# Weight loads of channels 64 apart, contiguous selection and a carry on either engine in a kernel of a long convolution and a routed two-token FFN

## The chip, the cores and the metric

The kernel runs on one core of one Trainium2 chip. The metric is the time of one execution on the device in microseconds (us), the median of several runs. A profile is one further execution, taken by the hardware profiler. Engines: PE multiplies matrices (PEld loads its weights, PEq is its sequencer), DVE and ACT do elementwise work, POOL and SP here mostly issue DMAs; SPq and ACTq are the queues on which SP and ACT issue theirs. L947 means line 947 of the kernel before.

## The reference

Cut to what matters; all arrays are bf16, x is 2048 tokens of 512 channels.

```python
g = sigmoid((x * gate_w).sum(-1, keepdims=True))
# A: a state-space layer, 512 channels of 128 states each
dt = exp(log_dt)[:, None]; A = A_re + 1j*A_im; B = B_re + 1j*B_im; C = C_re + 1j*C_im
l = arange(2048).astype(bf16)                       # lags are rounded to bf16
P = exp((dt * A)[:, :, None] * l[None, None, :])
K = einsum("dn,dnl,dn->dl", C, P, dt * B).real
a = causal_convolution(x, K) + x * Dskip            # over tokens, by channel
# B: the two tokens with the largest r go through a gated FFN
r = x @ w_r; idx = argsort(-r)[:, :2]; xs = x[idx]
b = x;  b[idx] += ((silu(xs @ w_gate) * (xs @ w_up)) @ w_down) * sigmoid(r[idx])
out = g * a + (1 - g) * b
```

## The kernel before, in words

The convolution runs in the frequency domain, over two blocks (b = 0, 1) of 1024 tokens and two halves (h = 0, 1) of HC = 256 channels. Its steps, with the lines of the profile:

- **Head.** The parameters are loaded; `scaled` (L598) multiplies them on PE by a diagonal of exp(log_dt). The results that it writes `wide` (AL and tb) have channels in natural order in PSUM: four matmuls, each writing every fourth column. DVE makes from them the phases (TMP1, TMP2, B16) and the products of B and C (CM1, CM2, WW). The first DVE operation that needs the last parameter, B_im, is CM1. `warm` (L640) is filler work on PE.
- **Tokens.** x is loaded (U), transposed (XT) and folded, and `forward` (L947) multiplies it by the tables F to get its spectrum X. The routing and the FFN (L813 to L912) lie between; a scatter by POOL (L916) adds its result to a copy of x in the output tensor, from which U is loaded again later.
- **Tables.** The exponential of A dt times a lag is a product of one of 32 factors (t1) and one of NJ = 21 factors (t2). `tab1` builds the first (TP, sines by ACT at L471 in eight passes per half; `quarter`, `first` and `step` on PE prepare their angles, and one `SCL`, L479, negates the sine of each of four angle groups); `tab2` the second (RW), on DVE.
- **Taps.** `kgen` (L966) multiplies, for four channels at a time, a weight load of 32 t1 x 4 channels with 21 t2 x 4 channels, 64 such groups per half. Of the 4 x 4 pairs of channels only the equal ones are wanted. Groups are gathered in PSUM and copied to KA (`EV`, L475) in pieces of 12, 12, 8, 12, 12 and 8 groups; KA has a group's 21 x 4 columns side by side.
- **Selection.** `sel` and `sel2` (L978 to L994) pick the equal channels: for each of the four channels of a group (c4) a matmul with columns of an identity reads every 84th element of KA (64 of them, or two sets of 64) and writes every fourth column of PSUM, on four 32-column tiles of PE side by side. L982 adds the rows of Dskip and of the FFN; L994 takes a few edge taps. The result, KC, is in natural channel order.
- **Spectra.** `kspec` (L1015) multiplies KC by tables KP, giving KK for tap block i = 0 (four matrices u) and i = 1 (one). Block 1 needs a carry: block 0's spectrum is added, or subtracted. For the first half PE adds it by matmuls behind the product (L1017, chosen by `CARRY = (0,)`); for the second, ACT writes it into PSUM ahead of the product (L1009).
- **Products and inverse.** DVE multiplies X by KK and combines (L460, `products`; for one part PE adds, L1053). `inverse` (L1100) turns the result back, into PSUM banks which ACT has filled with the skip term (L1078); L1110 and L1118 scale the result into U, which goes out by DMA.

What sets the order: no engine schedules itself. `ORDER` is one list of all operations, by three-digit numbers in base 36 in the order in which the program defines them; each engine runs its own in that order and waits by semaphores for what they depend on, DMA issues included. `SECOND` has a digit for each operation that can run on either of two engines (`EV`, `SCL` and others), `PLACES` the PSUM bank or buffer of each short-lived tile. The `cost=` figures have no effect on the running kernel.

## Time and profile before

| | us |
|---|---|
| median of 3 runs (151.97 to 153.57) | 152.06 |
| the profiled execution | 150.95 |
| its span, first to last instruction | 149.1 |
| busy in it: PE / PE weight loads | 140.9 / 104.1 |
| busy in it: DVE / ACT / POOL | 137.8 / 127.1 / 30.1 |

The span is shorter than the execution by what lies before the first and after the last instruction. A row of a timeline is start, duration, engine, line, operation, out<-in, count, and in brackets the idle time ahead of it with what ended it; neighbours on one engine overlap by some 0.1 us, since the pipeline takes the next before the last has drained. A row of a group is line, engine, operation, shapes, count, then busy us and mean ns of one, then idle time ahead and its causes. A row of the chain of waits is start, us, and what ran or was waited for. TensorE had its full clock (mean granted clock 0.996).

### The profile page before, as it was taken

To read this page: it belongs to the slowest core of one execution; us is meant where nothing else is said; L and a number is where in the kernel's file an instruction comes from. 1 tells how busy PE (TensorE), PEld (TensorE's weight loads), DVE (VectorE), ACT (ScalarE), POOL (GpSimd) and SP (SyncE) were. 2 spreads that over 40 slices of the span, in tenths; PEclk is the share of its full clock that TensorE was granted. 3 is DMA by queue.
4 is the path that set the end of the run, shared out by engine and by line. 5 is a ranking of instruction groups with operands and counts; after the bars stand their busy time and mean duration, and the time that the engine had idled before them with its cause. 6 is when DMAs were issued, how large, how long until landed. Compare 5 with 4: busy or idle time off the path is not lost.

```text
span 149.1 us, 3990 instructions
## 1 busy us (share of the span) xinstructions
PE 140.9 (94%) x1717; PEld 104.1 (70%) x1733; DVE 137.8 (92%) x192; ACT 127.1 (85%) x198; POOL 30.1 (20%) x11
## 2 busy tenths in 40 slices
PE   7889998999999999999989999999999999999990
PEld 2767755486664445968747879987886688888880
DVE  0699998999999999999999699999999999999982
ACT  3497989999999999999996986595999999999521
POOL 2000200000000999999930000000000000000000
PEclk9999999999999999999999999999999999999998
DMA  4899599919900004000491000558920011114314
GB/s 130 264 320 373 160 407 429 364 27 303 457 7 0 0 4 141 0 4 0 110 418 45 0 0 4 156 180 321 392 87 0 4 35 39 46 29 141 104 37 141
DMA packets 12499, 21.16 MB, mean 142 GB/s; under 512 B 1175, under 2 KB 8354, under 8 KB 12322
## 3 DMA queue, kind: packets, MB, share of 16 engines
q1 hardware_dynamic: 11474, 20.26, 38.7%
q10 hardware_dynamic: 976, 0.66, 1.4%
q8 instruction: 13, 0.21, 0.6%
q14 instruction: 4, 0.03, 0.1%
q0 software_dynamic: 32, 0.00, 0.0%
HBM read 18.81 MB, written 4.20 MB: 154 GB/s over the span
## 4 chain that ended last, share of the span: by engine, by line
PE 69%; ACT 13%; DVE 10%; DMA 4%; issue 1%; SPq 1%
PE ps L1100 18%; PE ps L947 14%; PE ps L966 8%; DVE AR L460 8%; PE ps L1015 7%; ACT AR L475 5%; ACT AR L471 5%; PE ps L699 3%; PE ps L978 3%; DMA AR<-in_A_B_im_dram 3%; PE ps L892 2%; DMA AR<-in_A_log_dt_dram 2%; DVE AR L475 2%; PE ps L704 2%; PE ps L994 1%; PE ps L1053 1%
## 5 line engine op out<-in xcount | busy, mean ns | idle before, releaser
L460 DVE TENSOR_TENSOR AR<-AR 128x1024 bf16<-128x1024 bf16 (+8 forms) x135 | 118.1, 932 | 5.3 <-ACT AR L471 3.6
L475 ACT ACTIVATE AR<-ps 128x1024 bf16<-128x1024 f32 (+9 forms) x60 | 51.7, 880 | 9.4 <-PE ps L966 3.1
L916 POOL DMA_INDIRECT out_dram<-AR x1 | 27.8, 27805 | 32.2 <-DVE AR L464 32.2
L947 PE MATMUL ps<-AR 128*128 128x512 bf16 x121 | 29.3, 379 | 0.5
L471 ACT ACTIVATE AR<-ps 128x1024 bf16<-128x1024 int16 (+2 forms) x34 | 28.2, 871 | 1.7 <-PE ps L598 1.6
L1100 PE MATMUL ps<-AR 128*128 128x256 bf16 x256 | 29.4, 273 | 0.0
L1100 PEld LDWEIGHTS ps<-AR 128*128 128x128 bf16 x256 | 24.8, 98 | 3.7 <-DVE AR L460 0.4
L947 PEld LDWEIGHTS ps<-AR 128*128 128x128 bf16 x128 | 11.9, 97 | 12.5
L966 PEld LDWEIGHTS ps<-AR 128*128 128x128 bf16 x512 | 18.6, 96 | 1.9
L1015 PE MATMUL ps<-AR 128*128 128x256 bf16 x160 | 19.0, 273 | 0.0
L966 PE MATMUL ps<-AR 128*128 128x84 bf16 (+1 forms) x512 | 18.9, 196 | 0.0
L471 ACT ACTIVATE ps<-AR 128x256 f32<-128x256 bf16 (+1 forms) x36 | 17.8, 554 | 0.1
L1015 PEld LDWEIGHTS ps<-AR 128*128 128x128 bf16 x160 | 15.5, 98 | 2.5 <-ACT ps L471 0.4
L479 ACT ACTIVATE AR<-AR 128x256 int32<-128x256 f32 (+2 forms) x22 | 13.1, 635 | 0.1
L471 ACT ACTIVATE AR<-AR 128x1024 bf16<-128x1024 int16 (+4 forms) x12 | 9.4, 782 | 1.3 <-DMA AR<-in_A_log_dt_dram 1.3
L1110 ACT ACTIVATE AR<-ps,AR 128x256 bf16<-128x256 f32 x24 | 9.9, 490 | 0.0
L640 PE MATMUL ps<-AR 128*128 128x464 bf16 x22 | 6.7, 444 | 0.9 <-DVE AR L643 0.9
L460 DVE TENSOR_TENSOR AR<-AR,ps 128x2048 bf16<-128x2048 bf16 (+1 forms) x6 | 7.2, 1257 | 0.3 <-PE ps L598 0.3
L699 PE MATMUL ps<-AR 128*128 128x512 f16 x24 | 6.2, 380 | 0.0
L1118 ACT ACTIVATE AR<-ps,AR 128x256 bf16<-128x256 f32 x3 | 1.4, 474 | 5.1 <-PE ps L1100 4.2
L978 PE MATMUL ps<-AR 128*32 128x128 bf16 x64 | 4.7, 420 | 0.2 <-ACT AR L475 0.2
L475 DVE COPY AR<-ps 128x1024 bf16<-128x1024 bf16 (+1 forms) x8 | 4.8, 679 | 0.0
(76 smaller groups left out, 98.7 us busy)
## 6 DMA issues: line engine op xcount, KB each, us to landing
AR<-c_ksp SPq DMA_DIRECT2D x5, 512.0 KB, 4.9
AR<-in_A_u_dram SPq DMA_DIRECT2D x8, 256.0 KB, 5.0
AR<-out_dram SPq DMA_DIRECT2D x4, 512.0 KB, 7.1
AR<-c_inv SPq DMA_DIRECT2D x1, 2048.0 KB, 8.8
AR<-in_B_w_up_dram SPq DMA_DIRECT2D x1, 1792.0 KB, 7.0
AR<-in_B_w_gate_dram SPq DMA_DIRECT2D x1, 1792.0 KB, 14.1
out_dram<-AR SPq DMA_DIRECT2D x14, 128.0 KB, 2.2
AR<-c_fwd SPq DMA_DIRECT2D x2, 512.0 KB, 6.7
```

Of the source, the lines that this page charges most:

```text
L460: return P.op(DVE, lambda h: h.tensor_tensor(out=o, in0=a, in1=b, op=op), rd, wr, cost=tt_cost(o, a, b), **k)
L471: return P.op(ACT, lambda h: h.activation(out=o, in_=a, func=func, scale=scale, bias=bias), rd, wr, cost=0.185 + nel(o) * 0.833e-3 + (0.09 ...
L475: return P.op((ACT, DVE), (lambda h: h.activation(out=o, in_=a, func=ACTF.Copy), lambda h: h.tensor_copy(o, a)), rd, wr, cost=(0.185 + n * ...
L479: return P.op((ACT, DVE), (lambda h: h.activation(out=o, in_=a, func=ACTF.Copy, scale=c), lambda h: h.tensor_scalar(out=o, in0=a, scalar1= ...
L699: r = hh.matmul(pb(0, 128, b * 512, (1, 512)), TI(4), PC(0, 128, k * D + h * HC, (0, 2), (1, HC)), start=False, stop=True, skip_group_chec ...
L916: P.op(POOL, lambda h: h.indirect_dma_start(dr(out, 0, (D, L), (1, D)), bass.IndirectOffsetOnAxis(ap=IDX(0, 2, 0, (1, 1)), axis=0), ZB(0, ...
L947: last = h.matmul(pb(0, 128, j * 512, (1, 512)), F[ft](0, 128, (kt * 2 + 1 - j) * 128, (1, 128)), pm[q](0, 128, kt * 512, (1, 512)), start ...
L966: last = hh.matmul(pb(0, 128, g // k * 512 + g % k * W4 + o, (1, n)), TP[h][1 - i // 2](0, 128, (b0 + g) * 128, (1, 128)), r[i](0, 128, (b ...
L978: last = hh.matmul(pb(32 * k, 32, c4, (256, 2), (4, 64)), CB(0, 128, c4, (4, 32)), ka(c4, GROUPS[2 * bk][k], (16, 2)), start=(c4 == 0), st ...
L1015: last = hh.matmul(pb(0, 128, n * 256, (1, 256)), KP[u](0, 128, tau * 128, (1, 128)), KC[h](0, 128, jg * 256, (1, 256)), start=(k == 0 and ...
L1100: r = hh.matmul(pb(0, 128, e * 256, (1, 256)), G(0, 128, ((par * 2 + part) * 4 + ft) * 512 + (2 * t2 + e) * 128, (1, 128)), X(0, 128, h * ...
L1110: return [hh.activation(out=U(0, 128, tb * D + h * HC, (1, HC)), in_=pb(0, 128, tb // 2 % 2 * 256, (1, HC)), func=ACTF.Copy, scale=SG(0, 1 ...
```

## The change

- `scaled`, where `wide`: a half's channels are laid out in PSUM so that the four of a group (a weight load) are 64 apart in the half, not neighbours. All tables follow; `WT` makes the products WW in two operations per part instead of one, reading in the new order.
- `kgen`: eight pieces of eight groups instead of six; the copy to KA writes with a step of four elements, so that the rows of four groups lie side by side.
- `sel`, `sel2`: read runs of four elements, and write 64 contiguous columns. The Dskip and FFN rows are one matmul of 256 columns instead of four of 64.
- `kspec`: the carry is an operation of its own ahead of the product, on ACT or on PE for each of the eight cases. By the new list PE does two of the first half's four and three of the second's.
- The two loads of F (512 KB each) become four (256 KB each).
- A new list of all operations, with other choices of engine and place. Decoded, among others: the log_dt load is SP's first; DVE has five of the eight transposes' copies instead of six; both quarter turns of the first half's second table run on ACT; one of the four block-0 spectra of the first half and three of that half's four block-1 products come behind the first part of the second half's `kgen`; the first half's inverse takes block 0 before block 1.

```diff
-CARRY = (0,)
...
-            DQ([(F[2 * j](0, 128, 0, (1, 2048)), f_c[:, j * 2048:(j + 1) * 2048])], [], [F[2 * j], F[2 * j + 1]], 524288)
+            for f in (2 * j, 2 * j + 1):
+                DQ([(F[f](0, 128, 0, (1, 1024)), f_c[:, f * 1024:(f + 1) * 1024])], [], [F[f]], 262144)
...
-                        o = out(k, (4, 128)) if wide else out(k * 128, (1, 128))
+                        o = out(4 * k, (HC, 2), (1, 4), (16, 16)) if wide else out(k * 128, (1, 128))
...
-        n4 = lambda b, c: b(0, 128, c, (1, 128), (128, 4))
-        w4 = lambda b, c: b(0, 128, c, (4, 128), (1, 4))
+        def WT(p, b0, b1, op):
+            def f(hh):
+                r = None
+                for h in range(2):
+                    n4 = lambda b, c: b(0, 128, c + 64 * h, (1, 16), (128, 4), (16, 4))
+                    r = hh.tensor_tensor(out=WW(0, 128, p * D + h * HC, (1, HC)), in0=n4(*b0), in1=n4(*b1), op=op)
+                return r
+            P.op(DVE, f, [CM1, CM2], [(WW, p)], cost=1.38)
...
-        TT(w4(WW, 0), n4(CM1, 0), n4(CM2, D), ALU.subtract, [CM1, CM2], [(WW, 0)])
-        TT(w4(WW, D), n4(CM1, D), n4(CM2, 0), ALU.add, [CM1, CM2], [(WW, 1)])
+        WT(0, (CM1, 0), (CM2, D), ALU.subtract)
+        WT(1, (CM1, D), (CM2, 0), ALU.add)
...
-            for b0, ng in ((0, 12), (12, 12), (24, 8), (32, 12), (44, 12), (56, 8)):
+            for b0, ng in [(8 * i, 8) for i in range(8)]:
...
-                EV(KA[h](0, 128, b0 * W4, (1, ng * W4)), pb(0, 128, 0, (512, 2), (1, k * W4)), [pb], [(KA[h], b0)])
-            ka = lambda c4, j, *d: KA[h](0, 128, c4 + 4 * j, *d, (4 * NJ, 64))
+                EV(KA[h](0, 128, b0 * W4, (4 * W4, ng // 4), (1, 4), (4, W4)), pb(0, 128, 0, (512, 2), (1, k * W4)), [pb], [(KA[h], b0)])
+            ka = lambda c4, j, *d: KA[h](0, 128, (c4 + 4 * j) * 4, *d, (4 * W4, 16), (1, 4))
...
-                            last = hh.matmul(pb(32 * k, 32, c4, (256, 2), (4, 64)), CB(0, 128, c4, (4, 32)), ka(c4, GROUPS[2 * bk][k], (16, 2)),
+                            last = hh.matmul(pb(32 * k, 32, 64 * c4, (256, 2), (1, 64)), CB(0, 128, c4, (4, 32)), ka(c4, GROUPS[2 * bk][k], (64, 2)),
                                              start=(c4 == 0), stop=(c4 == 3 and bk + k > 0), tile_position=(0, 32 * k))
                     if bk == 0:
-                        for c4 in range(4):
-                            last = hh.matmul(pb(0, 32, c4, (4, 64)), CB(0, 128, 64, (1, 32)), ZB(0, 128, h * HC + c4, (4, 64)), start=False, stop=(c4 == 3), tile_position=(0, 0))
+                        last = hh.matmul(pb(0, 32, 0, (1, HC)), CB(0, 128, 64, (1, 32)), ZB(0, 128, h * HC, (1, HC)), start=False, stop=True, tile_position=(0, 0))
...
-                        last = hh.matmul(pb(32 * k, 32, c4, (4, 64)), CB(0, 128, c4, (4, 32)), ka(c4, GROUPS[4][k]), start=(c4 == 0), stop=(c4 == 3), tile_position=(0, 32 * k))
+                        last = hh.matmul(pb(32 * k, 32, 64 * c4, (1, 64)), CB(0, 128, c4, (4, 32)), ka(c4, GROUPS[4][k]), start=(c4 == 0), stop=(c4 == 3), tile_position=(0, 32 * k))
...
-                        last = hh.matmul(pb(0, 128, 256 + c4, (4, 64)), CB(0, 128, EK0 + (c4 * 2 + k) * 32 - 32, (1, 128)), ka(c4, 1 - k), start=False, stop=True, skip_group_check=True)
+                        last = hh.matmul(pb(0, 128, 256 + 64 * c4, (1, 64)), CB(0, 128, EK0 + (c4 * 2 + k) * 32 - 32, (1, 128)), ka(c4, 1 - k), start=False, stop=True, skip_group_check=True)
...
-                        pe = h in CARRY
-                        pb = psum(2, full=True, seed=i == 1 and not pe)
+                        pb = psum(2, full=True, seed=i == 1)
...
-                        if i and not pe:
-                            AC(pb(0, 128, 0, (1, 1024)), KK[h](0, 128, (1 - part) * 2048 + qd * 1024, (1, 1024)), ACTF.Copy, [ck], [pb], scale=1.0 - 2.0 * part)
+                        if i:
+                            kc = lambda m, n, part=part, qd=qd: KK[h](0, 128, (1 - part) * 2048 + qd * 1024 + m * 512, (1, n))
+                            def carry(hh, pb=pb, part=part, kc=kc):
+                                return [hh.matmul(pb(0, 128, m * 512, (1, 512)), CB(0, 128, 128 * part, (1, 128)), kc(m, 512), start=True, stop=False, skip_group_check=True) for m in range(2)][-1]
+                            def seed(hh, pb=pb, part=part, kc=kc):
+                                return hh.activation(out=pb(0, 128, 0, (1, 1024)), in_=kc(0, 1024), func=ACTF.Copy, scale=1.0 - 2.0 * part)
+                            P.op((ACT, PE), (seed, carry), [ck, CBI], [pb], cost=(0.185 + 1024 * 0.833e-3, 0.4314))
...
-                            for m in range(2 * i * pe):
-                                last = hh.matmul(pb(0, 128, m * 512, (1, 512)), CB(0, 128, 128 * part, (1, 128)), KK[h](0, 128, (1 - part) * 2048 + qd * 1024 + m * 512, (1, 512)), start=False, stop=True, skip_group_check=True)
```

More of the change, by code (lines that the diff above doesn't have):

```diff
@@ L397 @@
 )
 PLACES = (
[L399 removed]
+    "21044600176014706064110140224111440010012400106222606064020266000140240220010664642246010100000001010260606201160066220615052430260022023470456"
 )
@@ L1014, in ks @@
                                     jg = KUSE[u][1]
-                                    last = hh.matmul(pb(0, 128, n * 256, (1, 256)), KP[u](0, 128, tau * 128, (1, 128)), KC[h](0, 128, jg * 256, (1, 256)), start=(k == 0 and n % 2 == 0 and (pe or i == 0)), stop=(k == len(uses) - 1 and n % 2 == 1 and not (i and pe)), skip_group_check=(i == 1))
-                            for m in range(2 * i * pe):
-                                last = hh.matmul(pb(0, 128, m * 512, (1, 512)), CB(0, 128, 128 * part, (1, 128)), KK[h](0, 128, (1 - part) * 2048 + qd * 1024 + m * 512, (1, 512)), start=False, stop=True, skip_group_check=True)
+                                    last = hh.matmul(pb(0, 128, n * 256, (1, 256)), KP[u](0, 128, tau * 128, (1, 128)), KC[h](0, 128, jg * 256, (1, 256)), start=(k == 0 and n % 2 == 0 and i == 0), stop=(k == len(uses) - 1 and n % 2 == 1), skip_group_check=(i == 1))
                             return last
-                        P.op(PE, ks, [KP[u] for u in uses] + [(KC[h], KUSE[u][1]) for u in uses] + ([CBI, ck] if i and pe else []), [pb.buf], cost=4 * len(uses) * 0.1095 + 2 * i * pe * 0.2157)
+                        P.op(PE, ks, [KP[u] for u in uses] + [(KC[h], KUSE[u][1]) for u in uses], [pb.buf], cost=4 * len(uses) * 0.1095)
                         o = KK[h](0, 128, i * 4096 + part * 2048 + qd * 1024, (512, 2), (1, 512))
```

41 lines of the change are left out of this document (20 added, 21 removed).

## The prediction

> **What bounds the kernel now.** I read the busy time by stage first (columns: start and end of the stage, its length, then busy us of PE, of its weight loads, of DVE, ACT and POOL, the granted clock, DMA share, GB/s).
>
> ```profile
> 20.00:59.00 39.00, 38.08 (x403) 22.19 (x407) 38.35 (x74) 38.77 (x59) 10.77 (x1) 1.00 0.51 191
> 59.00:75.40 16.40, 15.87 (x286) 11.96 (x288) 16.40 (x25) 16.05 (x19) 16.40 (x1) 1.00 0.15 46
> 75.40:85.43 10.03, 9.91 (x109) 7.27 (x111) 8.86 (x12) 8.50 (x14) 0.63 (x1) 1.00 0.34 139
> 85.43:143.29 57.86, 57.60 (x701) 48.93 (x703) 57.31 (x57) 48.76 (x87) 0.52 (x1) 1.00 0.30 102
> ```
>
> Up to 75.4 all three compute engines are full; from there ACT has room, PE and DVE have none, and DVE's last product ends at 143.29. So nothing is won by easing one engine alone. Up to 75 the question is ACT's queue; behind it, whichever of PE and DVE ends later. Next I read the timelines at the joints, ACT first, then DVE.
>
> ```profile
> 15.16 1.02 ACT L475 ACTIVATE AR<-ps 128x1024 bf16<-128x1024 bf16 x1 [1.04 <-PE ps L797]
> 19.76 0.20 ACT L475 ACTIVATE AR<-ps 128x32 bf16<-128x32 f32 x1 [0.68 <-PE ps L820]
> 82.24 1.02 ACT L475 ACTIVATE AR<-ps 128x1024 bf16<-128x1024 f32 x1 [1.42 <-PE ps L1015]
> 83.16 1.02 ACT L471 ACTIVATE AR<-ps 128x1024 bf16<-128x1024 int16 x1
> 84.06 0.39 ACT L475 ACTIVATE AR<-ps 128x256 bf16<-128x256 f32 x1
> 84.33 1.07 ACT L479 ACTIVATE AR<-AR 128x1024 bf16<-128x1024 bf16 x1
> ```
>
> ```profile
> 8.51 1.22 DVE L460 TENSOR_TENSOR AR<-AR,ps 128x1024 f32<-128x1024 bf16 x1 [0.33 <-PE ps L598]
> 85.43 10.57 DVE L460 TENSOR_TENSOR AR<-AR 128x2048 bf16<-128x2048 bf16 x7 [1.17 <-ACT AR L479]
> ```
>
> The four ACT rows from 82.24 are neighbours: an operation costs its duration less about 0.1 (82.24 to 83.16 is 0.92). DVE's one large idle, 1.17 before 85.43, waits for the negated sine of the second half's last angle group (84.33), and ACT is late there because the evacuation ahead of it stood 1.42 waiting for PE. I call 85.43 the joint.
>
> **The head.** The log_dt load goes from third to first on SP's queue.
>
> ```profile
> 0.73 0.36 SPq L482 DMA_DIRECT2D AR<-c_bf  x1
> ```
>
> ```profile
> 1.65 2.57 DMA AR<-in_A_log_dt_dram
> 4.24 3.79 DMA AR<-in_A_B_im_dram
> 8.07 0.41 PE ps L598 x4
> ```
>
> It is issued 1.65 - 0.73 = 0.92 earlier, and so are the exp that waits for it and the B_im load that ACT issues behind that exp: landing at 7.1. But the new order puts both B groups behind that landing, not one (another 0.41). CM1 starts at 8.51 - 0.92 + 0.41 = 8.0: head 0.5, of which I take 0.4. The two halved F loads add two issues of about 0.4 on SP, ahead of the constants it loads next; PE meets F3 only behind the logits, so I cost this at nothing, and 0.8 if that cover fails. The "wide" results go to PSUM 64 bytes apart instead of 16.
>
> ```profile
> L598 PE MATMUL ps<-AR x24: 219/314/314, 5.2 to 8.3; 128*128 128x128 bf16 x24
> ```
>
> Spaced writes already cost 314 against 219 for the contiguous eight of the 24. I take no change; the bounds are 16 times 0.095 = 1.5 either way.
>
> **The selection (L978 to L994).** PE's rows for the first half, with matmuls to compare:
>
> ```profile
> 75.46 1.15 PE L978 MATMUL ps<-AR 128*32 128x128 bf16 x16 [0.15 <-ACT AR L475]
> 76.66 1.15 PE L978 MATMUL ps<-AR 128*32 128x128 bf16 x13
> 78.71 0.68 PE L991 MATMUL ps<-AR 128*32 128x64 bf16 x16
> 79.32 1.13 PE L994 MATMUL ps<-AR 128*128 128x64 bf16 x8
> 17.04 1.75 PE L813 MATMUL ps<-AR 128*128 128x2 bf16 x64
> 93.62 5.66 PE L966 MATMUL ps<-AR 128*128 128x84 bf16 x160
> ```
>
> ```profile
> L978 PE MATMUL ps<-AR 128*32 128x128 bf16 x64 | 4.7, 420 | 0.2 <-ACT AR L475 0.2
> L966 PE MATMUL ps<-AR 128*128 128x84 bf16 x256 | 18.6, 199 | 0.0
> ```
>
> A half costs 75.46 to 77.81 and 78.71 to 80.45, together 4.1. A 128-column selection takes 420 ns, where the contiguous L598 took 219: of the 201 extra, the spaced write explains 95, and the read, one element every 168 bytes, is left with about 106. The change makes the write contiguous and the read one of four-element runs; L966 reads such runs, and its 84 columns take 199, no more than 219 for 128 suggests. So both penalties should go, and what is left is an issue rate: between 1.75/64 = 27 and 5.66/160 = 35 ns each. 32 + 16 + 8 matmuls at 27 to 35 ns are 1.5 to 2.0; one 256-column product (0.11) and two pipeline tails of about 0.15 make it 1.9 to 2.4. I take 2.2, a saving of 1.9 per half; the bounds are nothing (the access keeps its price) and 2.2.
>
> The Trainium skill, Advanced Engine Details and Errata, Memory Cachelines, says that SBUF wants two hits on a 16-byte line and PSUM two neighbouring fp32 for full rate; by it the sum is the same, the spaced "wide" writes stay slow, and the 314 agrees.
>
> **ACT ahead of the last KA evacuation of the first half.** The order list, decoded, gives the operations in front. Prices:
>
> ```profile
> L475 ACT ACTIVATE AR<-ps 128x1024 bf16<-128x1024 bf16 x2 | 2.1, 1052 | 1.0 <-PE ps L797 1.0
> L678 ACT ACTIVATE AR<-AR 128x1024 int32<-128x1024 int32 x3 | 3.2, 1082 | 0.0
> L479 ACT ACTIVATE AR<-AR 128x512 bf16<-128x512 bf16 x3 | 1.9, 630 | 0.0
> L479 ACT ACTIVATE AR<-AR 128x256 int32<-128x256 f32 x13 | 5.3, 433 | 0.0
> L475 ACT ACTIVATE AR<-ps 128x1008 bf16<-128x1008 f32 x8 | 8.1, 1009 | 3.2 <-PE ps L966 3.1
> L475 ACT ACTIVATE AR<-ps 128x672 bf16<-128x672 f32 x4 | 2.9, 727 | 0.1
> ```
>
> Each less 0.1. Taken over from DVE: one token transpose 0.95, one quarter turn (L678) 0.98, one table negation 0.53, two tiny copies 0.2; a third, pulled in front, 0.1; given to DVE: two angles, -0.66. Eight evacuations of 672 for four of 1008 and two of 672: 8 x 0.63 - 4 x 0.91 - 2 x 0.63 = 0.14. Pulled in front: a sine 0.92 and a negation 0.97. Sum +4.1. Against it stand the head's 0.4 and the idle of 1.04 and 0.68 in the early rows; the new order strews exponentials between ACT's PE-dependent copies, so I take 1.2 of the 1.7. The last KA evacuation comes 2.5 later; bounds 2.0 and 3.7.
>
> **PE from there to the end.**
>
> ```profile
> 80.45 1.75 PE ps L1015 x16
> 89.18 0.43 PE ps L1017 x2
> ```
>
> ```profile
> 89.45 3.47 PE L966 MATMUL ps<-AR 128*128 128x84 bf16 x96
> 140.06 5.41 PE L1100 MATMUL ps<-AR 128*128 128x256 bf16 x48
> ```
>
> Now: 75.46 to 89.45 is 14.0, then 56.0 to 145.47. After: selection 2.2, a quarter turn 0.43, three block-0 spectra of 1.75, one carry and its product 0.87: 8.8. Behind it the second half gains the fourth spectrum 1.75, two more block-1 products 0.88, one of them with its carry 0.43, a product without carry 0.44, loses two with carry 1.74, loses 1.9 of selection, and gains three carries moved to PE, 1.3: 56.0 + 1.2 = 57.2. So 66.0 where 70.0 stood, 4.0 less, from a start 2.5 later: PE ends 1.5 earlier. ACT loses three carries and gains two, in a stage where it has 9 us to spare: nothing.
>
> **DVE.**
>
> ```profile
> L475 DVE COPY AR<-ps 128x1024 bf16<-128x1024 bf16 x7 | 4.7, 746 | 0.0
> L678 DVE TENSOR_SCALAR AR<-AR 128x1024 int32<-128x1024 int32 x1 | 0.7, 672 | 0.0
> L479 DVE TENSOR_SCALAR AR<-AR 128x256 int32<-128x256 f32 x3 | 1.0, 348 | 0.0
> L460 DVE TENSOR_TENSOR AR<-AR 128x512 bf16<-128x512 f32 x2 | 2.5, 1244 | 0.0
> ```
>
> Ahead of the joint it gives away 0.65 (copy), 0.57 (turn) and some 0.5 (negation, tiny copies), takes two angles, 0.5, and splits each WW product in two (1244 now; about 0.12 more each, bounds -0.4 and +0.6): -1.0; head -0.4; reordering about -0.3 ahead and +0.3 behind. Ready at 84.26 - 1.7 = 82.6. ACT's negation: in front of it stand the 4.1 without the two pulled operations (1.9, in front in both), without one spectrum evacuation 0.92 and one negation 0.53 that now come later: +0.8; the wait of 1.42 in front of that evacuation goes too, the head 0.4, idle 1.2. It starts at 84.33 - 2.2 = 82.1 and ends at 83.2. DVE goes on there, 2.2 earlier, with 0.3 more to do: 1.9 earlier. The later of the two engines decides: **1.5 earlier**. The tail is built as before. The profiled execution took 150.95 (span 149.1, 1.85 around it), the median of the runs is 152.06, 1.11 above; so 149.45 by the profile and 150.5 as a median.
>
> **The rivals.** *All idle goes*: 1.7 of ACT's idle and 2.2 of each selection. PE: 4.1 - 0.4 - 1.7 = 2.0 later, 4.6 shorter, -2.6; DVE goes on at its own 82.6, -2.5. Time 149.5. For it: the idle is all waiting for PE. *ACT gives it back*: no early idle goes; the last KA comes 3.7 later and PE ends 0.3 earlier, 151.8. For it: ACT is full from 20 to 75.4 and is given 2.2 of new work there. *The selection keeps its price* (slower): runs of four don't help, because only whole contiguous rows do, or the price is in the 32-column weights. Then PE's path is 3.8 longer: -1.5 + 3.8 = +2.3, 154.4. It decides from the point where a half saves less than 1.15. Against it: L966's 199. *ACT's spaced store*: KA is now written one element every 8 bytes, which no row of ACT shows. The nearest spaced access is WW's on DVE, 1244 ns for 512 float pairs;
>
> ```profile
> L460 DVE TENSOR_TENSOR AR<-AR 128x512 f16<-128x512 f32 x1 | 0.8, 806 | 0.0
> ```
>
> contiguous it is 806, a factor of 1.54. 727 times that is 0.39 more on each of eight, 3.1 in front of the joint: +1.6, 153.7. A gain is excluded, as the elements stay the same; I take nothing, by the nearest row, ACT's own 727 for these elements. By the line rule of the Trainium skill's SBUF — State Buffer (SBUF: two separate sides) two stores fall in each line and the price is nothing; no run here shows it yet.
>
> **How the numbers follow.** Forecast 0.44, all idle goes 0.20, ACT gives it back 0.14, selection 0.12, store 0.10. One per cent, 1.5 us, is about what a measurement of this kernel tells from no change. The forecast's own range is 149.9 to 151.3, a little more than half of it (0.25) below 150.54; with the first rival faster is 0.45; the rest of the forecast and the second rival are 0.33; slower is 0.22. The range reaches down past the first rival to 149.0 and up over the store's 153.7 to 153.8, and leaves out the selection's 154.4 and a little below.
>
> **What would show it.** Right: selection matmuls near 220 ns and a half near 2.2; KA evacuations of 672 still near 727; DVE's wait before the second half's last angle group under 1 us; the second half's L966 starting near 87 and the last L1100 ending near 144. Wrong: L978 above 300 ns; KA evacuations above 900; PE idle by several us near 78, where it would wait for ACT; DVE idle anywhere behind the joint, which this sum has at nothing and which the new order of reloads and spectra could bring.

## The result, and the profile after

The changed kernel takes 159.24 us (median of 4 runs, 158.25 to 160.47) against 152.24 for the kernel before: a ratio of 1.0445 with a 95% interval of 1.0338 to 1.0553, 6.8 us slower. The forecast was 150.5 with a range up to 153.8. Here and below the ratios leave disturbed runs out, while the medians are over all runs, so the two can differ by some tenths of a us. The profiled execution is the slowest of the four (160.47, span 158.6), so times are taken from the ratios, and the profile is read for what waits for what. In the kernel after, L474 is what was L475 (copies), L478 was L479 (scaled copies, the negation among them), L459 was L460 (DVE's products), L972 was L966, L984 to L999 were L978 to L994 (the selection), L1024 was L1015 and L1107 was L1100.

The busy time by stage, for the same four stretches of time and with the same columns as before (PE, its weight loads, DVE, ACT, POOL):

```profile
20.00:59.00 39.00, 38.54 (x410) 21.25 (x407) 38.39 (x75) 38.89 (x60) 5.78 (x1) 1.00 0.43 158
59.00:75.40 16.40, 14.03 (x212) 9.06 (x211) 14.75 (x20) 16.37 (x17) 8.26 (x1) 1.00 0.07 26
75.40:85.43 10.03, 6.55 (x109) 4.19 (x108) 7.97 (x11) 10.03 (x10) 0.00 (x0) 1.00 0.59 208
85.43:143.29 57.86, 53.48 (x717) 44.73 (x710) 51.84 (x49) 55.52 (x84) 0.52 (x1) 1.00 0.25 86
```

Until 59 little has changed. Between 59 and 85.43 ACT alone is full: PE, which had 15.87 and 9.91 busy, has 14.03 and 6.55. The costliest groups, shapes kept apart (busy us, mean ns of one, then the idle time in front of them and what ended it), show why:

```profile
L474 ACT ACTIVATE AR<-ps 128x672 bf16<-128x672 f32 x16 | 25.9, 1748 | 0.0
L984 PE MATMUL ps<-AR 128*32 128x128 bf16 x64 | 1.6, 231 | 3.1 <-ACT AR L474 3.1
L972 PE MATMUL ps<-AR 128*128 128x84 bf16 x256 | 19.6, 200 | 3.7 <-ACT AR L474 3.3 <-DVE AR L459 0.4
```

A KA copy of 672 elements, 727 ns before, takes 1748: 1.02 more on each of 16. The selection did fall, from 420 to 231 ns, but PE now stands 3.1 in front of it, for KA. The chain of waits, by engine, was PE's to 69% before; it is ACT's now:

```profile
ACT 54%; PE 34%; DVE 5%; issue 3%; DMA 2%; SPq 1%; ACTq 0%
```

ACT's and DVE's timelines where the copies stand (start, length, what, how many, and in brackets the idle time before):

```profile
62.99 1.74 ACT L474 ACTIVATE AR<-ps 128x672 bf16<-128x672 f32 x1
82.03 3.19 ACT L474 ACTIVATE AR<-ps 128x672 bf16<-128x672 f32 x2
89.19 1.06 ACT L478 ACTIVATE AR<-AR 128x1024 bf16<-128x1024 bf16 x1
```

```profile
73.39 1.09 DVE L459 TENSOR_TENSOR AR<-AR 128x1792 bf16<-128x1792 bf16 x1 [0.58 <-ACT AR L478]
76.31 3.83 DVE L459 TENSOR_TENSOR AR<-AR 128x2048 bf16<-128x2048 bf16 x4 [1.82 <-ACT AR L478]
81.30 7.11 DVE L459 TENSOR_TENSOR AR<-AR 128x2048 bf16<-128x2048 bf16 x9 [1.16 <-ACT AR L478]
90.28 1.23 DVE L459 TENSOR_TENSOR AR<-AR 128x2048 bf16<-128x2048 bf16 x1 [1.88 <-ACT AR L478]
113.10 0.42 DVE L459 TENSOR_TENSOR AR<-ps,AR 8x256 bf16<-8x256 f32 x1 [3.57 <-ACT AR L474]
```

ACT's KA copies between 96.2 and 110, as a group:

```profile
L474 ACT ACTIVATE AR<-ps 128x672 bf16<-128x672 f32 x8 | 12.6, 1752 | 0.0
```

Eight copies stand between 62.99 and 85.2, among the sines and negations of the second half's tables. The negations that come after them are later, and DVE waits for four of them: 0.58 + 1.82 + 1.16 + 1.88 = 5.4. The joint, which was at 85.43, is at 90.28. The other eight stand behind it, from 96.30 to 109.74, and DVE waits 3.57 at 113.10 for a copy that ACT makes behind them.

### The profile page after: what moved, and what is told of

Its sections match the earlier page's. It is cut to its first block, busy times and chain, and to the rows that moved or that the text cites. A ratio compares the mean times of both kernels' runs of the same rounds, so it can differ in the third digit from the quotient of the medians.

```text
span 158.6 us, 4010 instructions
## 1 busy us (share of the span) xinstructions
PE 141.5 (89%) x1729; PEld 102.5 (65%) x1729; DVE 136.8 (86%) x190; ACT 141.5 (89%) x205; POOL 16.3 (10%) x11
## 4 chain that ended last, share of the span: by engine, by line
ACT 54%; PE 34%; DVE 5%; issue 3%; DMA 2%; SPq 1%; ACTq 0%
ACT AR L474 27%; PE ps L1107 17%; ACT AR L470 15%; ACT AR L478 6%; PE ps L1024 6%; DVE AR L459 4%; PE ps L598 2%; PE ps L1060 2%; ACT AR L684 2%; DMA AR<-in_A_A_im_dram 2%; PE ps L803 1%; ACT ps L1017 1%; PE ps L1015 1%; PE ps L646 1%; PE ps L972 1%
## 5 line engine op out<-in xcount | busy, mean ns | idle before, releaser
L459 DVE TENSOR_TENSOR AR<-AR 128x1024 bf16<-128x1024 bf16 (+7 forms) x133 | 116.1, 928 | 9.6 <-ACT AR L478 5.4
L474 ACT ACTIVATE AR<-ps 128x1024 bf16<-128x1024 f32 (+7 forms) x67 | 67.3, 1072 | 0.9 <-PE ps L1060 0.5
L470 ACT ACTIVATE AR<-ps 128x1024 bf16<-128x1024 int16 (+2 forms) x34 | 29.2, 923 | 4.6 <-PE ps L598 4.6
L953 PE MATMUL ps<-AR 128*128 128x512 bf16 x128 | 30.3, 379 | 0.8 <-ACT AR L474 0.8
L1107 PE MATMUL ps<-AR 128*128 128x256 bf16 x256 | 29.1, 273 | 0.0
L1107 PEld LDWEIGHTS ps<-AR 128*128 128x128 bf16 x256 | 25.0, 98 | 3.2
L972 PE MATMUL ps<-AR 128*128 128x84 bf16 (+1 forms) x512 | 20.1, 197 | 3.7 <-ACT AR L474 3.3
L972 PEld LDWEIGHTS ps<-AR 128*128 128x128 bf16 x512 | 18.8, 97 | 6.3 <-ACT AR L474 4.5
L1024 PE MATMUL ps<-AR 128*128 128x256 bf16 x160 | 19.1, 273 | 1.2 <-ACT AR L474 1.2
L1024 PEld LDWEIGHTS ps<-AR 128*128 128x128 bf16 x160 | 15.3, 98 | 4.3 <-ACT AR L474 1.4
L922 POOL DMA_INDIRECT out_dram<-AR x1 | 14.0, 14032 | 37.9 <-DVE AR L459 37.9
L470 ACT ACTIVATE ps<-AR 128x256 f32<-128x256 bf16 x32 | 14.0, 481 | 0.0
L478 ACT ACTIVATE AR<-AR 128x256 int32<-128x256 f32 (+2 forms) x21 | 13.1, 660 | 0.1
L459 DVE TENSOR_TENSOR AR<-AR,ps 128x2048 bf16<-128x2048 bf16 (+1 forms) x6 | 7.2, 1212 | 0.9 <-PE ps L598 0.9
L710 PE MATMUL ps<-AR 128*128 128x512 bf16 x16 | 4.8, 383 | 1.5 <-ACT AR L470 1.4
L803 PE MATMUL ps<-AR 128*128 128x128 bf16 x64 | 4.6, 219 | 0.6 <-ACT AR L474 0.5
```

Of the source, the lines that this page charges most:

```text
L459: return P.op(DVE, lambda h: h.tensor_tensor(out=o, in0=a, in1=b, op=op), rd, wr, cost=tt_cost(o, a, b), **k)
L470: return P.op(ACT, lambda h: h.activation(out=o, in_=a, func=func, scale=scale, bias=bias), rd, wr, cost=0.185 + nel(o) * 0.833e-3 + (0.09 ...
L474: return P.op((ACT, DVE), (lambda h: h.activation(out=o, in_=a, func=ACTF.Copy), lambda h: h.tensor_copy(o, a)), rd, wr, cost=(0.185 + n * ...
L478: return P.op((ACT, DVE), (lambda h: h.activation(out=o, in_=a, func=ACTF.Copy, scale=c), lambda h: h.tensor_scalar(out=o, in0=a, scalar1= ...
L922: P.op(POOL, lambda h: h.indirect_dma_start(dr(out, 0, (D, L), (1, D)), bass.IndirectOffsetOnAxis(ap=IDX(0, 2, 0, (1, 1)), axis=0), ZB(0, ...
L953: last = h.matmul(pb(0, 128, j * 512, (1, 512)), F[ft](0, 128, (kt * 2 + 1 - j) * 128, (1, 128)), pm[q](0, 128, kt * 512, (1, 512)), start ...
```

## The experiments

Two theories were on record before the first runs: S, the store of KA at a step of 8 bytes is the cost; O, the new order and the head are. The first four kernels ran on one chip.

**The store in runs.** KA keeps its new layout; ACT reads PSUM at a step of 84 floats instead and stores contiguously.

```diff
- EV(KA[h](0, 128, b0 * W4, (4 * W4, ng // 4), (1, 4), (4, W4)), pb(0, 128, 0, (512, 2), (1, k * W4)), ...
+ EV(KA[h](0, 128, b0 * W4, (4 * W4, ng // 4), (4, W4), (1, 4)), pb(0, 128, 0, (512, 2), (1, W4), (W4, 4)), ...
```

> The changed kernel, with KA in its new layout but the copy walking it the other way: it reads PSUM with a step of 84 floats and stores contiguously. Theory S (the store with a step of 8 bytes is what costs: 16 copies at 1748 ns where 727 stood, eight of them ahead of the joint): a copy of 672 falls to 730 to 800 ns, the selection stays at 231 ns, and the time falls to 150 to 153 us. Theory O (the new order and the longer head are what costs, the copies would be hidden by ACT's slack): the copies fall too, but the time stays above 156. If ACT pays as much for a spaced read of PSUM, the copies stay above 1400 ns, the time stays near 158 to 159, and the run tells nothing about S against O.

Measured: 151.32, ratio 0.9907 (0.9866 to 0.9947), which is 8.2 us below the changed kernel by the ratios. S holds. The profiled execution, 149.45, is the fastest of the ten. The groups of this kernel, its PE timeline at the first selection, and, on ACT, the negation in front of the joint and a later wait:

```profile
L474 ACT ACTIVATE AR<-ps 128x672 bf16<-128x672 f32 x16 | 11.4, 742 | 2.0 <-PE ps L972 2.0
L984 PE MATMUL ps<-AR 128*32 128x128 bf16 x64 | 1.6, 230 | 0.0
```

```profile
76.30 0.50 PE L984 MATMUL ps<-AR 128*32 128x128 bf16 x17
78.19 0.43 PE L999 MATMUL ps<-AR 128*128 128x64 bf16 x8
80.06 5.40 PE L1024 MATMUL ps<-AR 128*128 128x256 bf16 x48 [1.44 <-DMA AR<-c_ksp]
86.16 0.71 PE L972 MATMUL ps<-AR 128*128 128x84 bf16 x16
99.94 5.84 PE L1024 MATMUL ps<-AR 128*128 128x256 bf16 x52
107.08 1.92 PE L1024 MATMUL ps<-AR 128*128 128x256 bf16 x16 [1.31 <-ACT AR L474]
139.35 4.53 PE L1107 MATMUL ps<-AR 128*128 128x256 bf16 x40
```

```profile
80.45 1.06 ACT L478 ACTIVATE AR<-AR 128x1024 bf16<-128x1024 bf16 x1
105.61 0.48 ACT L470 ACTIVATE ps<-AR 128x256 f32<-128x256 bf16 x1 [1.64 <-DMA AR<-out_dram]
```

The copies cost 742 again (727 in the kernel before, 743 in the next kernel, both contiguous), though they now read PSUM one float every 336 bytes: the spaced read is free, the spaced store is not. The selection is untouched by it. New in this trace are two waits that the prediction did not have: PE's 1.44 for the spectra's constants at 80.06, and, behind ACT's 1.64 for a reload, PE's 1.31 at 107.08.

**KA as before.** The changed kernel with KA's old layout: contiguous copies, and a selection that reads one element every 168 bytes but still writes contiguously.

```diff
- ka = lambda c4, j, *d: KA[h](0, 128, (c4 + 4 * j) * 4, *d, (4 * W4, 16), (1, 4))
+ ka = lambda c4, j, *d: KA[h](0, 128, c4 + 4 * j, *d, (4 * NJ, 64))
```

> The changed kernel with KA as it was before (a group's columns side by side, copied contiguously), so that the selection again reads one element every 168 bytes but still writes contiguously. S: copies at 727 ns, time 150.5 to 153. O: above 156. In both the selection matmul of 128 columns shows what the read alone costs: 231 of now plus about 106, some 330 ns, if read and write prices add; near 231 if the write was the whole price, near 420 if the read was.

Measured: 151.05, ratio 0.9937 (0.9914 to 0.9961). Its groups, and PE where the first selection stands:

```profile
L474 ACT ACTIVATE AR<-ps 128x672 bf16<-128x672 f32 x16 | 11.4, 743 | 1.8 <-PE ps L972 1.8
L984 PE MATMUL ps<-AR 128*32 128x128 bf16 x64 | 4.4, 421 | 0.0
```

```profile
76.23 1.15 PE L984 MATMUL ps<-AR 128*32 128x128 bf16 x16
79.50 1.13 PE L999 MATMUL ps<-AR 128*128 128x64 bf16 x8
80.44 5.42 PE L1024 MATMUL ps<-AR 128*128 128x256 bf16 x48
97.63 1.37 PE L984 MATMUL ps<-AR 128*32 128x128 bf16 x17
102.74 7.61 PE L1024 MATMUL ps<-AR 128*128 128x256 bf16 x68
```

With the write contiguous and the read spaced, a selection still takes 421 ns, where both spaced took 420. The read alone sets that price; nothing of it was the write. Beyond that, this kernel keeps the selection's price and is nevertheless not slower than the kernel before. What the cheap selection is worth is therefore small: 0.5 us between this ratio and the last, with overlapping intervals. Where it goes is taken up below.

**Wide results in runs of four.** The head's "wide" products write runs of four floats, and the diagonal is read at a step of 32 bytes to make the order come out.

```diff
- o = out(4 * k, (HC, 2), (1, 4), (16, 16)) if wide ...; DG(0, 128, k * 128, (1, 128))
+ o = out(4 * k, (HC, 2), (16, 16), (1, 4)) if wide ...; DG(0, 128, k * 128, (64, 2), (1, 16), (16, 4)) if wide ...
```

> The changed kernel with the wide results of the head written in runs of four floats, the diagonal being read with a step of 32 bytes instead. The wide matmuls started every 233 ns in the changed kernel. S and O both: if the 64-byte step of the write is the price, they come down to 60 to 120 ns and CM1 starts about 1.3 us earlier, so the time falls by 0.5 to 1.5 us; if the spaced read of the moving operand costs as much, nothing changes. The KA copies stay at 1748 ns, so S has the time still above 156.

Measured: 161.0, ratio 1.0609 (1.0578 to 1.064), where a gain of 0.5 to 1.5 was expected, or none: a miss. Its L598, and PE's first eight of them beside the same eight in the kernel with the store in runs:

```profile
L598 PE MATMUL ps<-AR x24: 285/397/397, 4.7 to 9.3; 128*128 128x128 bf16 x24
4.66 1.92 PE L598 MATMUL ps<-AR 128*128 128x128 bf16 x8 [0.65 <-DVE AR L459]
```

```profile
4.79 1.05 PE L598 MATMUL ps<-AR 128*128 128x128 bf16 x8 [0.59 <-DVE AR L459]
```

1.92 where 1.05 stood, at a granted clock of 1.00: a matmul takes 397 ns instead of 314. This points to the spaced read of the moving operand costing more than the spaced write that it replaces. It is one execution, and the first eight take up to 1.89 in other executions too (see the last section), but there with weight loads of some 232 ns; here none is above 152. What the edit does to the time is not shown: from 7 to 10 the granted clock of this profile was 0.52, in the four runs it was 0.974 to 0.986 on average, and CM1 starts at 9.75, while it starts at 9.88 in the profile of the changed kernel.

**Only the channel order.** The kernel before, with its own order, pieces and KA layout, and of the change only the channels 64 apart and the selection's contiguous writes.

```diff
- last = hh.matmul(pb(32 * k, 32, c4, (256, 2), (4, 64)), CB(0, 128, c4, (4, 32)), ka(...
+ last = hh.matmul(pb(32 * k, 32, 64 * c4, (256, 2), (1, 64)), CB(0, 128, c4, (4, 32)), ka(...
```

> The kernel before, in its own order and with its own pieces and KA layout, given only the channels 64 apart and the selection's contiguous writes (and what goes with them: the wide results 64 bytes apart, WW in halves, one Dskip matmul). S: no loss, 150.5 to 153.5: selection near 330 ns (1 us less of PE in each half), against it about 1 us later in the head. O: the same, since the order is the old one; above 156 would speak against both and for the layout of channels itself.

Measured: 152.07, ratio 0.9999 (0.9975 to 1.0023). No change. The selection was expected near 330 ns; it shows again that the write is not its price:

```profile
L984 PE MATMUL ps<-AR 128*32 128x128 bf16 x64 | 4.4, 420 | 0.1
```

The next four asked what the store's price depends on, and which of the 16 copies carry the time.

**Two groups side by side, and eight.** In the layout, 4 is replaced by 2 (a store every 4 bytes, runs of two for the selection) or by 8 (every 16 bytes, runs of eight).

```diff
- EV(KA[h](0, 128, b0 * W4, (4 * W4, ng // 4), (1, 4), (4, W4)), ...
+ EV(KA[h](0, 128, b0 * W4, (n * W4, ng // n), (1, n), (n, W4)), ...      n = 2, n = 8
- ka = lambda c4, j, *d: KA[h](0, 128, (c4 + 4 * j) * 4, *d, (4 * W4, 16), (1, 4))
+ ka = lambda c4, j, *d: KA[h](0, 128, (c4 + 4 * j) * n, *d, (n * W4, 64 // n), (1, n))
```

> The changed kernel with two groups side by side instead of four: ACT stores one element every 4 bytes, and the selection reads runs of two elements, 4 bytes, one run every 336 bytes. Three theories of the store's price, all from 742 ns contiguous and 1748 at a step of 8 bytes. Step theory, the elements' part of the price grows with the bytes that a store moves on: half of the growth is kept, KA copies near 960 to 1080, 16 x 0.3 = 5 us of ACT where 16 were, time near 153. Run theory, any store whose neighbour in the row is not the next element pays the full price: copies stay at 1748, time near 159. Line theory, two stores in a 16-byte line are too few but four suffice: copies at 742, time near 151. For the read: if whole runs of 8 bytes are needed, the selection's L984 goes back to 421; if a run of two is enough, it stays at 231; halves give 326.

> The changed kernel with eight groups side by side: ACT stores one element every 16 bytes, one in each 16-byte line; the selection reads runs of eight, 16 bytes. Step theory: twice the growth again, KA copies near 2750 to 3300, time near 168 to 172. Run theory: copies stay at 1748, time near 159. Line theory, by stores that fall in a line: half the rate once more, copies near 3300. The selection's L984 stays at 231 if a run of four already brought all there is, and falls to about 220 if not.

Measured: 151.73, ratio 0.9946 (0.9909 to 0.9983), with pairs; 186.71 in a single run with eights. The copies with pairs and the selection behind them, then the copies with eights:

```profile
L474 ACT ACTIVATE AR<-ps 128x672 bf16<-128x672 f32 x16 | 14.5, 955 | 1.1 <-PE ps L972 1.0
L984 PE MATMUL ps<-AR 128*32 128x128 bf16 x64 | 2.6, 310 | 0.5 <-ACT AR L474 0.5
```

```profile
L474 ACT ACTIVATE AR<-ps 128x672 bf16<-128x672 f32 x16 | 49.5, 3360 | 0.5 <-PE ps L972 0.5
```

| step of the store | ns for 672 elements | 16-byte stretches that a copy visits |
|---|---|---|
| 2 bytes (contiguous) | 742 | 84 |
| 4 bytes | 955 | 168 |
| 8 bytes | 1748 | 336 |
| 16 bytes | 3360 | 672 |

From 4 bytes on, each further stretch costs the same: (1748 - 955) / 168 = 4.7 ns and (3360 - 1748) / 336 = 4.8. All three lie on about 150 + 4.75 ns a stretch; contiguous, 150 + 84 x 4.75 = 549 lies under the 742 that the elements take anyway. The step theory for pairs (960 to 1080) and the line theory for eights (near 3300) came close; that four in a line would be free, and that the price does not depend on the step, fall. The 186.71 are far above the 168 to 172 of the step theory; the granted clock of that run was 0.908 on average. For the read of the selection: 421 ns for runs of one element, 310 for two, 230 for four; runs of eight take 222 in the second half, at a granted clock of 1.00 (310 in the first half, where the clock was 0.50).

The Trainium skill, Advanced Engine Details and Errata, Memory Cachelines, asks for two hits on a 16-byte SBUF line for full rate. The 1748 ns, at two stores in such a line, disagree, and so do the 955 at four; the measurements decide.

**Only the first half spaced.** The second half's copies store in runs.

```diff
+ if h == 0:
      EV(KA[h](0, 128, b0 * W4, (4 * W4, ng // 4), (1, 4), (4, W4)), ...
+ else:
+     EV(KA[h](0, 128, b0 * W4, (4 * W4, ng // 4), (4, W4), (1, 4)), ...
```

> The changed kernel with the spaced store in the first half's eight KA copies alone; the second half's are stored in runs and read PSUM at the step, as in the kernel that took 151.3. The 7.9 us between that kernel and the changed one are to be divided. Theory J, the one the prediction's store rival was sized by: the eight copies of the first half stand in ACT's full queue ahead of the joint and carry most of it, 8 x 1.02 = 8.1 of ACT's time less what idle takes up there, so 5 to 6 of the 7.9: 156 to 157. Theory K: the second half's seven copies in a row, 7.4 us on ACT with PE's second-half kernel generation and DVE waiting behind them, carry most: then this run is at 152 to 153.5.

Measured: 157.08, ratio 1.0365 (1.0297 to 1.0433). By the ratios that is 0.0458 x 152.1 = 7.0 above the store in runs, for eight copies that cost ACT 8 x 1.02 = 8.2 more; the second half's eight add 0.0080 x 152.1 = 1.2, within the intervals. DVE's rows ahead of the joint, and the negation:

```profile
71.74 1.09 DVE L459 TENSOR_TENSOR AR<-AR 128x1792 bf16<-128x1792 bf16 x1 [0.59 <-ACT AR L478]
74.66 3.83 DVE L459 TENSOR_TENSOR AR<-AR 128x2048 bf16<-128x2048 bf16 x4 [1.82 <-ACT AR L478]
79.65 7.10 DVE L459 TENSOR_TENSOR AR<-AR 128x2048 bf16<-128x2048 bf16 x9 [1.17 <-ACT AR L478]
89.09 1.22 DVE L459 TENSOR_TENSOR AR<-AR 128x2048 bf16<-128x2048 bf16 x1 [2.33 <-ACT AR L478]
```

```profile
88.00 1.06 ACT L478 ACTIVATE AR<-AR 128x1024 bf16<-128x1024 bf16 x1
```

The negation starts at 88.00 where it was at 80.45 with the store in runs: 7.6 of the 8.2 arrive there. DVE's waits, 0.59 + 1.82 + 1.17 + 2.33, come to 5.9. Theory J holds, and somewhat more strongly than it was sized. (The "seven copies in a row, 7.4 us" of theory K are three copies of KA and four others; the second half's eight copies stand between 96.30 and 109.74.)

**One copy on DVE.** One of the second half's KA copies is given to DVE (one digit of the list of second choices).

> The changed kernel with one of the second half's KA copies on DVE instead of ACT, with the same spaced store. It measures what DVE pays for the same access. If the price sits in the memory that is written, DVE pays it too: 672 floats from PSUM cost DVE about 0.85 contiguous by its 0.69 for 512, so near 1.9 us. If it sits in ACT, near 0.85 to 0.9. The time may move by 1 either way; one look cannot tell that.

Measured: 160.02 in a single run. DVE's row in the groups:

```profile
L470 DVE CAST AR<-ps 128x672 bf16<-128x672 f32 x1 | 1.7, 1694 | 3.6 <-PE ps L968 3.6
```

1694 on DVE, 1748 on ACT: the price is that of the store, not of one engine. No run has a contiguous copy of 672 on DVE; the 0.85 us of the expectation are an estimate from its 0.69 for 512.

**The same layout, stored two by two.** Each copy becomes two of 336 elements, each writing two neighbours, skipping two, and so on, with the two groups read 84 floats apart.

```diff
- EV(KA[h](0, 128, b0 * W4, (4 * W4, ng // 4), (1, 4), (4, W4)), pb(0, 128, 0, (512, 2), (1, k * W4)), ...
+ def two(hh, b0=b0, pb=pb):
+     return [hh.activation(out=KA[h](0, 128, b0 * W4 + 2 * i, (4 * W4, 2), (4, W4), (1, 2)),
+             in_=pb(0, 128, 2 * i * W4, (512, 2), (1, W4), (W4, 2)), func=ACTF.Copy) for i in range(2)][-1]
```

> The changed kernel with the same layout of KA, stored in another order: each copy becomes two of 336 elements, each of which writes two neighbouring elements (4 bytes), skips 4 bytes, and goes on. Every 16-byte line then takes four elements in succession, but every second store is followed by a gap. What is to be told apart is what the price counts, after 742, 955, 1748 and 3360 ns for steps of 2, 4, 8 and 16 bytes. Line count: the three spaced prices lie on 150 + 4.75 ns for each 16-byte line that a copy visits (168, 336 and 672 visits); here 84 visits for 336 elements, so 150 + 400 = 550 ns. Gap count: each step that is not to the next element costs the same; 168 gaps for 336 elements, 150 + 168 x 4.75 = 950. Contiguous 336 would be 150 + 336 x 0.88 = 446. Time between 152 and 160; two copies more per piece cost ACT a fixed 0.1 to 0.2 each.

Measured: 151.92 in a single run, with the layout of the kernel that takes 159.24. Its copies:

```profile
L977 ACT ACTIVATE AR<-ps 128x336 bf16<-128x336 f32 x32 | 12.5, 479 | 1.6 <-PE ps L972 1.6
```

479 ns. The count of gaps (950) falls. The count of stretches gave 550, 70 too many; contiguous was put at 446. So something close to the number of stretches visited is paid for, and the order of the stores decides, not the layout; the exact law stays open.

**The F loads in pairs again,** on the kernel with the store in runs:

```diff
- for f in (2 * j, 2 * j + 1):
-     DQ([(F[f](0, 128, 0, (1, 1024)), f_c[:, f * 1024:(f + 1) * 1024])], [], [F[f]], 262144)
+ DQ([(F[2 * j](0, 128, 0, (1, 2048)), f_c[:, j * 2048:(j + 1) * 2048])], [], [F[2 * j], F[2 * j + 1]], 524288)
```

> The kernel with the store in runs (151.3), with the two F loads joined in pairs again as in the kernel before: two DMA issues less on SP. The prediction cost the split at nothing, and at 0.8 if its cover fails. If it was right, the time stays within 0.5 of 151.3. If the split costs (two issues of 0.4 ahead of the constants), 150.5. A third theory: the pairs make PE wait, as F3 now lands with F2's load and F0 with F1's; then PE's forward matmuls wait near 20 us and the time is not better.

Measured: 151.38, ratio 0.9915 (0.9868 to 0.9961), against 0.9907. No cost of the split is seen, as predicted; the two intervals leave up to 0.9 us open either way.

**The first constants on ACT's queue,** again on the kernel with the store in runs:

```diff
- DQ([(CB(0, 128, 0, (1, 256)), cb_c[:, 0:256])], [], [(CB, "i")], 65536)
+ DQ([(CB(0, 128, 0, (1, 256)), cb_c[:, 0:256])], [], [(CB, "i")], 65536, eng=ACT)
```

> The kernel with the store in runs (151.3), with the first constants (c_bf, the diagonal's factor) loaded first on ACT's queue instead of second on SP's. In its profile the exp of log_dt ran at 3.09, but DVE's diagonal waited for c_bf until 4.04. Theory: the head is on the path, and the diagonal 0.5 earlier brings 0.3 to 0.5: 150.8 to 151.0. Rival: the head's next wait (A_re, one place later on ACT's queue, or the token loads on SP that PE waits for at 9.97) takes it up: no change, 151.3.

Measured: 149.61, ratio 0.9836 (0.9805 to 0.9867). This kernel is faster than the one before by 1.6%. DVE's diagonal starts at 3.68 instead of 4.04, and the first forward products 0.4 earlier than the 18.78 of the kernel with the store in runs:

```profile
3.68 0.69 DVE L447 TENSOR_TENSOR AR<-AR 128x512 bf16<-128x512 bf16 x1 [2.82 <-ACT AR L458]
18.34 1.02 PE L941 MATMUL ps<-AR 128*128 128x512 bf16 x4
80.19 2.02 PE L1012 MATMUL ps<-AR 128*128 128x256 bf16 x17 [1.99 <-ACT AR L458]
```

CM1, though, starts at 7.88 instead of 7.71, behind products that wait 0.35 for B_im. And at 80.19 the spectra (L1012 here) start where they did at 80.06: the 0.4 is lost there, in a wait that has grown. The two profiled spans say the same, 147.9 against 147.6. That the ratio is lower by 0.7% is thus not explained by the head, and the two intervals touch; what it owes to this edit stays open.

**The last forward group earlier,** on top of that, to see what the wait at 80 is. Only the order list changes: the second four matmuls of the first half's last forward group stand behind the first four.

> Where the first half's selection gain went. In the kernel with the store in runs the selection of the first half is 2.0 shorter than in the kernel with KA as before (76.30 to 78.6 against 76.23 to 80.4), but the spectra behind it start only 0.4 earlier (80.06 against 80.44), after a wait of 1.44 for the spectra's constants, c_ksp. These four loads are issued on SP when PE has done its last forward group (72.6), as they overwrite its input. This kernel is the one with the constants on ACT's queue, and of the last forward group (of 8 matmuls, which stand in two places) the second four stand directly behind the first four, ahead of two pieces of kernel generation and a turn: 2.3 earlier. Theory C, the wait is for the loads: the loads are issued 2 earlier, the spectra start near 78, the wait is gone. Theory D, DVE sets the end anyway (it does not stand still from 50 to 141): then the time is the same as without the move, 149.6, though the wait is gone; if PE sets it, 148 to 148.6. Theory E: the wait in front of the spectra is for something else (an evacuation on ACT, which the trace names in one of the two kernels): then it stays.

Measured: 148.92, ratio 0.9814 (0.9774 to 0.9853), the fastest kernel of the study, not told apart from 0.9836. The issue of the spectra's constants, PE at the selection and at the spectra, and the first row of DVE behind 50 us that has idle time in front of it:

```profile
71.16 1.76 SPq L469 DMA_DIRECT2D AR<-c_ksp  x4
```

```profile
77.47 0.50 PE L972 MATMUL ps<-AR 128*32 128x128 bf16 x18
79.53 5.40 PE L1012 MATMUL ps<-AR 128*128 128x256 bf16 x48
```

```profile
142.34 0.48 DVE L1113 TENSOR_SCALAR AR<-ps,AR 128x256 bf16<-128x256 f32 x1 [1.21 <-PE ps L1095]
```

The four loads are issued from 71.16 on, against 72.38 in the kernel without the move, and PE no longer waits in front of the spectra. They start 0.7 earlier (79.53 against 80.19), although in this execution the head's first products took 0.8 longer (1.89 against 1.05) and the selection comes 1.2 to 1.6 later. That agrees with theory C and speaks against E; the row of the last kernel that named ACT there most likely named the wrong engine. And DVE stands still nowhere between 50 and 142 (in the kernel without the move it waited 0.77 and 0.49), so, as D has it, not all of the wait could come back.

## Why the prediction was wrong

**The step that failed** is the price of the KA copies: "ACT's spaced store ... I take nothing, by the nearest row, ACT's own 727 for these elements", and in ACT's sum "Eight evacuations of 672 for four of 1008 and two of 672 ... = 0.14". The row of 727 is a contiguous store; it shares the number of elements with the new copy, and not what sets its price. The operation was rightly named as one that no row shows, the bound of 1.54 was taken from a spaced access of DVE, and then the lower bound was chosen. Measured is 1748 / 727 = 2.4, above both bounds: the 1.54 came from a spaced read on DVE, and what was to be bounded is a store.

The rest of that rival's mechanism was right: that its place is in front of the joint, and that the price arrives at the end nearly whole. With 1.02 in place of 0.39, its sum is -1.5 + 8 x 1.02 = +6.7; measured is +6.8. That they meet so closely is partly luck: by the run with the first half alone 7.0 of the 8.2 come from there, and the second half's eight copies, which the sum has at nothing, bring the other 1.2 by the ratios, though these two intervals overlap. The price, not the path, put the time outside the range.

**The rest of the forecast** can be read off the kernel with the store in runs, which is the change without that price: -1.4 by its ratio where -1.5 was forecast. That agreement is partly luck, by its parts:

- ACT's last KA copy of the first half, forecast 2.5 later, is 0.8 later (PE's selection starts at 76.30 instead of 75.46). ACT's busy time up to the end of that copy, the fourth busy time of each row below (the kernel before, then this one), shows why. Its work grew by 3.2, forecast 4.1; and of its idle 2.4 went (6.9 before, 4.55 here), forecast 1.6 with the head. The work handed over was oversized by 0.9, the idle undersized by 0.8.

```profile
0.00:75.41 75.41, 71.23 (x892) 46.18 (x903) 69.42 (x120) 68.51 (x98) 28.97 (x10) 1.00 0.50 177
0.00:76.25 76.25, 72.42 (x907) 45.80 (x907) 70.46 (x120) 71.70 (x105) 26.66 (x10) 1.00 0.50 174
```

- The selection, forecast 4.1 to 2.2, falls further, to 1.5, and the reason was half wrong. The two penalties of 95 and 106 do not add: with the write contiguous, the read alone still costs 421.
- PE's path between the halves, forecast 8.8, is 9.9 (the second half's L972 starts 86.16 instead of 87): the selection gives back 1.44 to the loads of c_ksp. They overwrite the input of the last forward group and are issued only behind it, in this kernel from 72.81 on, before from 71.89 on. The prediction moved the selection and the spectra, and did not follow the loads that the spectra wait for.
- PE's path from there, forecast 57.2, is 57.7, with a wait of 1.31 behind ACT's wait for the reload of U. "DVE idle anywhere behind the joint ... which the new order of reloads and spectra could bring" was looked for on DVE; it came on ACT and PE.
- PE ends at 143.88 instead of 145.47: 1.6 earlier, forecast 1.5. DVE's last product ends at 141.40 instead of 143.29: 1.9 earlier, as forecast.

So the selection, which carried the forecast with 1.9 per half, is worth 1.3 by the two profiled spans (148.9 with KA as before, 147.6 with the store in runs) and 0.5 by the ratios, out of 4.4 on PE: of the first half's 2.0, 1.6 goes to the constants, and of the second half's 2.4 (102.74 against 99.94, less the 0.4 before), 1.3 behind the reload. For the same reason the rival "the selection keeps its price", 154.4, was wrong in size: the kernel that is this rival, with KA as before, took 151.05.

**The head.** That the wide step of 64 bytes changes nothing holds (314 ns in the kernels with it, 314 before). The head came 0.8 earlier in the kernel with the store in runs (CM1 at 7.71), forecast 0.5. In the profiled execution of the changed kernel it came 1.4 later instead, for this:

```profile
L598 PE MATMUL ps<-AR x24: 219/502/502, 5.0 to 9.6; 128*128 128x128 bf16 x24
9.88 2.35 DVE L459 TENSOR_TENSOR AR<-AR,ps 128x1024 f32<-128x1024 bf16 x2 [0.88 <-PE ps L598]
```

The same matmuls took 219 to 314 throughout in the kernels with the store in runs and with only the channel order, so the edit alone is not the cause; the last section comes back to it. It may be one reason why this execution is the slowest of its four; the other three have no trace.

**Splitting the F loads** was costed at nothing, and no cost was seen.

**Signs.** "KA evacuations above 900" and "PE idle by several us near 78, where it would wait for ACT" both came, and say what they were meant to say. "L978 above 300" did not come.

## What to carry to other kernels

A layout that makes one operand cheap to read can make it dear to write: estimate the store by the stretches of memory that it visits in turn, not by its elements alone, and if the trace holds no such store, keep the whole range open instead of taking the row with the same number of elements. Put the step on the side where it is free (here the read from PSUM: 742 ns against 1748), and follow, for each step that comes earlier, the loads it waits for and what must end before they are issued.

## What the runs showed of the hardware that was not expected

- A store of two-byte elements on ACT at a step of 4, 8 and 16 bytes takes 955, 1748 and 3360 ns for 672 elements, contiguous 742; DVE pays 1694 at 8 bytes. It is the order of the stores that counts: the same addresses, two neighbours at a time, cost 2 x 479.
- ACT reads PSUM one float every 336 bytes at no extra cost (742 against 727).
- For a matmul, a spaced write to PSUM and a spaced read of the moving operand do not add. Runs of one, two, four and eight elements read at 421, 310, 230 and 222 ns for 128 columns; making the write contiguous beside the first changes nothing.
- The head's matmuls differ between executions with the same instructions there. In the changed kernel's profile most of the 24 took 502 ns, with weight loads of 230; in the kernel with KA as before, the one with the first half spaced and the one with the forward group earlier, the first few did (502 and 231 or 232 at most); in the kernel with the store in runs none did (314 and 139 at most). The granted clock reads 1.00 in these stretches all the same. Yet the matmuls there look like those at half clock: the head's transposes (L609, 128 contiguous columns each) took 312 ns with weight loads of 147 in the changed kernel's profile, and 219 with 98 in the kernel with the store in runs; in the kernel with wide results in runs of four, where the granted clock did read 0.50 from 7.2 to 10.4, the transposes of the tokens (L803) took 314 with 152. The Trainium skill, TensorE: Matmul & The Clock Gate, What's actually happening, has the array at half clock until a window of 3.4 us has been busy, and the window running free of the kernel, so that the moment of the switch moves. The change from 230 to 98 in the weight loads looks like that; the granted clock of these profiles does not show it, and no run here tested what sets the moment.
